# Where a tuned layer chain lets VectorE prepare its weights: a paced plan of conversions, later stores, an earlier first product

## The chip, the cores and the metric

One core of a Trainium2 chip runs the whole program. The metric is the device time of one launch in microseconds, as the median of several runs. Five compute engines work side by side: TensorE (PE, matmuls; PEld is its weight load), VectorE (DVE), ScalarE (ACT), GpSimd (POOL), and SyncE (SP), which here only issues DMAs. Each engine runs its instructions in the order in which the program emits them, so an instruction that waits holds back all behind it on its engine.

## The reference

The inputs are q, k, v of shape (4, 8, 576, 64) and the weights of two MLPs.

```python
scores = scale * np.matmul(q, k.transpose(0, 1, 3, 2))
Dmat = np.where(rel >= 0, gamma[:, None, None] ** rel[None, :, :], 0.0)
x = np.matmul(scores * Dmat, v)             # as (2304, 512): 4*576 tokens, 8*64 columns
h = x @ w_in                                # 512 -> 2048
x = (h * (1.0 / (1.0 + np.exp(-1.702 * h)))) @ w_out
h = x @ w2_in                               # 512 -> 1024
solu = h * softmax(h)
ln = (solu - mu) / np.sqrt(var + 1e-06) * g_ln
out = ln @ w2_out                           # 1024 -> 512
```

## The kernel before

**Stages.** The retention runs from 0 to 66 us in eight rounds k = 0 to 7 of two units each (a unit is a pair of heads of one batch). Then comes the first MLP in 24 steps, and from 492 us the second MLP, in which PE has no gaps.

**Numbers as pairs.** A float32 operand is held as a pair hi and lo, and a product takes three matmuls (hi·hi, lo·hi, hi·lo). `split` makes the pair: ACT casts the high part (L294 for weights, L628 for x), and POOL subtracts (L295, L630); for some of x's operands DVE subtracts (also L630).

**Products by sums.** A block product of two by two takes seven products, not eight. Their operands are sums: four of x's blocks (L285 and L621 on DVE) and four of the weights' blocks (L285, tiles t1 to t4). The results are put together by four additions with temporaries c11, c12, c21, c22 in `emit_h` (L678; copies L685 and L689 on ACT).

**Weights arrive as 64-bit words.** `convert` makes float32 of them with three DVE operations on 128x512 (L270, L273, L276). A raw slice is one DMA of SP's queue into one of two raw buffers.

**Steps.** The first MLP goes through four generations g of four slices of the hidden width, each with three pairs of token tiles and two halves i: step s = 6g + 2·(place of the pair) + i. A step is `emit_h` (seven products of six matmuls 128x384 in the order h_A, h_C, h_B, h_A, h_C, h_D, h_B, L672; `gate` gives g of h on ACT and DVE, L650 to L652) and `emit_y` (48 matmuls, 24 in steps 0 and 1, L736; added up by L745 from generation 1 on). The h products use four PSUM banks in turn, so each bank's last reader must be done before the next step's product of that name begins.

**x's operands.** A pair of tiles has seven operand tiles x0 to x6. In generation 0 the steps 1 and 3 make the next pair's (split of even j on POOL, of odd j on DVE) and store them to DRAM, xd; in the later generations steps 1 and 3 of each load them back, seven DMAs of 768 KB on ACT's queue, each after the product that frees its tile.

**The background list.** Conversions, sums and splits of weights for later steps stand in a list `bg`. `slot(n)` first runs up to three splits of the list `late` that an earlier slot took off, and then takes pieces of a summed cost of about n (a conversion operation costs 1) and emits them there. A step has one slot with a number in `emit_h`, after the adds of L678 and before the last two gates, and one after `emit_y`; the number is what is left over the slots left. At the end the list holds the second MLP's weights. `spill` splits such a slice into a park buffer (two in `ws`, three in `win[2]`) and stores it to DRAM, wd, on SP's queue, 512 KB each. After the last `emit_h`, `open_second` frees the first MLP's weights and fetches 14 slices of wd, and three more follow. `split_y` makes the second MLP's operands of the first token tiles from the finished y; in before it is called for the first pair after step 22.

**What sets the order.** There is no scheduler: the order of code is the order on each engine. The DMAs of SP and ACT share eight completion counters in turn, so a DMA also waits for the one that was issued eight places before it.

## Time and profile before

| What | Value |
|---|---|
| Runs | 692.77, 695.28, 695.31 us (median 695.28) |
| The profiled execution | 697.27 us, of it a span of 695.5 us |
| PE busy | 651.9 us, 94% |
| DVE, ACT, POOL busy | 485.6, 279.2, 213.2 us |
| Mean granted clock of PE | 0.973 |
| A step without a disturbance | 15.60 us |

The profile shows one execution. Busy times are summed per engine; since PE is busy for 94%, the places that matter are the few in which PE waits or runs at a lower clock. They lie between 66 and 112 us, near 150, 253, 350 and between 438 and 484 us.

### The profile page before, as it was taken

The numbers are of one execution on the slowest core, as the hardware profiler recorded it, in microseconds if no ns is written. First come the engines' busy times: TensorE is split into PE (matmuls) and PEld (weight loads), VectorE is DVE, ScalarE is ACT, GpSimd is POOL, SyncE is SP. The second block draws the span as 40 slices with busy tenths as digits, with TensorE's granted clock in tenths as the row PEclk, the third lists the DMA queues.
The fourth block names the chain that finished last, engine by engine and source line by source line (L and its number), as shares of the span: only waits on it lengthen the run. The fifth ranks groups of instructions, "written<-read, shape, count | busy, mean of one in ns | idle before, by whom it ended". The sixth has DMA issues, their size and how long they took to land.

```text
span 695.5 us, 11232 instructions
## 1 busy us (share of the span) xinstructions
PE 651.9 (94%) x4326; PEld 609.2 (88%) x4326; DVE 485.6 (70%) x846; ACT 279.2 (40%) x606; POOL 213.2 (31%) x216
## 2 busy tenths in 40 slices
PE   9999578989999989999999999589999999999998
PEld 8888478889999989999989999589888888888887
DVE  3897996675457766587767575565599878877780
ACT  3475344544444332333333334143354344442431
POOL 3489453540213110412111205052232234331300
PEclk9999878999999999999999999889999999999999
DMA  9997347181255762184952377767800000000001
GB/s 346 417 417 315 137 169 270 59 329 52 61 203 228 275 266 88 61 318 164 382 181 76 124 315 270 320 252 284 345 16 1 32 30 32 16 16 31 32 31 46
DMA packets 30006, 121.78 MB, mean 175 GB/s; under 512 B 3328, under 2 KB 3840, under 8 KB 29952
## 3 DMA queue, kind: packets, MB, share of 16 engines
q1 hardware_dynamic: 23760, 87.96, 33.4%
q10 hardware_dynamic: 6192, 33.10, 12.4%
q8 instruction: 34, 0.56, 0.3%
q14 instruction: 20, 0.16, 0.1%
HBM read 88.28 MB, written 32.77 MB: 174 GB/s over the span
## 4 chain that ended last, share of the span: by engine, by line
PE 68%; DMA 6%; DVE 4%; ACT 1%; issue 1%; POOL 0%; ACTq 0%; DVEq 0%
PE y L736 22%; PE o L890 14%; PE h L800 12%; PE h_B L672 5%; PE h_A L672 5%; PE h_C L672 5%; DMA x<-xd 4%; PE h_D L672 3%; PE zT L864 2%; DMA mem<-in_w2in 1%; DVE mem L273 1%; DVE mem L276 0%; DVE mem L270 0%; DVE x L630 0%; DVE g L652 0%
## 5 line engine op out<-in xcount | busy, mean ns | idle before, releaser
L295 POOL TENSOR_TENSOR win<-mem,win 128x256 fp32r<-128x256 f32 (+2 forms) x63 | 58.6, 960 | 114.7 <-ACT win L294 80.6
L736 PE MATMUL y<-g,wo 128*128 128x384 f32 x432 | 79.7, 339 | 0.0
L736 PEld LDWEIGHTS y<-g,wo 128*128 128x128 f32 x432 | 77.1, 192 | 0.3 <-DVE mem L745 0.2
L295 POOL TENSOR_TENSOR ws<-mem,ws 128x512 fp32r<-128x512 f32 (+1 forms) x28 | 32.1, 1157 | 103.0 <-ACT ws L294 103.0
L745 DVE TENSOR_TENSOR mem<-y,mem 128x384 f32<-128x384 f32 x72 | 36.7, 552 | 30.7 <-PE y L736 30.4
L678 DVE TENSOR_TENSOR mem<-h_B,mem 128x384 f32<-128x384 f32 x48 | 26.5, 551 | 32.3 <-PE h_B L672 30.2
L685 ACT COPY mem<-h_A 128x384 f32<-128x384 f32 x24 | 11.6, 483 | 84.7 <-PE h_A L672 84.7
L800 PE MATMUL h<-ut,win 128*128 128x512 f32 x168 | 42.9, 390 | 0.0
L890 PE MATMUL o<-u,zs 128*128 128x512 f32 (+1 forms) x171 | 41.7, 388 | 0.0
L736 PE MATMUL y<-g,wo1dt.float32r 128*128 128x384 f32 x216 | 40.3, 334 | 0.0
L736 PE MATMUL y<-g,wo0dt.float32r 128*128 128x384 f32 x216 | 40.3, 334 | 0.0
L806 DVE TENSOR_TENSOR mem<-h,mem 128x512 f32<-128x512 f32 x36 | 24.6, 687 | 22.4 <-PE h L800 12.5
L890 PE MATMUL o<-wo,zs 128*128 128x512 f32 (+1 forms) x171 | 40.0, 378 | 0.0
L630 POOL TENSOR_TENSOR x<-mem,x 128x384 fp32r<-128x384 f32 x30 | 34.6, 1180 | 17.5 <-ACT x L628 17.5
L736 PEld LDWEIGHTS y<-g,wo0dt.float32r 128*128 128x128 f32 x216 | 37.7, 188 | 0.0
L736 PEld LDWEIGHTS y<-g,wo1dt.float32r 128*128 128x128 f32 x216 | 37.7, 188 | 0.0
L800 PEld LDWEIGHTS h<-ut,win 128*128 128x128 f32 x168 | 31.4, 188 | 6.4
L672 PE MATMUL h_B<-x,win0dt.float32r 128*128 128x384 f32 x108 | 23.8, 358 | 13.7 <-DVE mem L678 10.8
L890 PEld LDWEIGHTS o<-wo,zs 128*128 128x128 f32 x171 | 31.0, 188 | 6.0
L276 DVE SCALAR_TENSOR_TENSOR mem<-mem 128x512 uint32<-128x512 uint32 x44 | 34.5, 785 | 1.2
L890 PEld LDWEIGHTS o<-u,zs 128*128 128x128 f32 x171 | 29.9, 189 | 5.1
L270 DVE TENSOR_SCALAR mem<-mem 128x512 uint32<-128x512 uint32 x44 | 20.7, 469 | 18.4 <-DMA mem<-in_w2in 10.6
(150 smaller groups left out, 1547.7 us busy)
## 6 DMA issues: line engine op xcount, KB each, us to landing
x<-xd ACTq DMA_DIRECT2D x42, 768.0 KB, 9.6
xd<-x SPq DMA_DIRECT2D x21, 768.0 KB, 5.3
mem<-in_w SPq DMA_DIRECT2D x28, 512.0 KB, 4.6
in<-in_att SPq DMA_DIRECT2D x16, 576.0 KB, 9.1
in<-in_att SPq DMA_DIRECT2D x16, 544.0 KB, 8.9
out<-mem SPq DMA_DIRECT2D x17, 256.0 KB, 2.0
mem<-in_w2out SPq DMA_DIRECT2D x8, 512.0 KB, 4.8
wd<-ws SPq DMA_DIRECT2D x8, 512.0 KB, 6.4
```

Source lines behind the costliest of these rows:

```text
L270: lambda: nc.vector.tensor_scalar(x, high, 3, 0x3FFFFFF8, ALU.logical_shift_left, ALU.bitwise_and),
L276: lambda: nc.vector.scalar_tensor_tensor(x, low, 29, high, ALU.logical_shift_right, ALU.bitwise_or),
L295: (engine or self.nc.gpsimd).tensor_tensor(lo, src, f32(hi), ALU.subtract)
L630: (engine or self.nc.gpsimd).tensor_tensor(x[:, 1, k], a[:, k], f32(x[:, 0, k]), ALU.subtract)
L672: nc.tensor.matmul(o, w[:, c:c + P], x[j][:, m, k], start=(start and i == 0), stop=(stop and i == 5), skip_group_check=True,)
L678: add = lambda o, a, b: nc.vector.tensor_tensor(o, a, b, ALU.add)
L736: nc.tensor.matmul(self.yps[m], w[:, c:c + P], gs[:, b], start=(begin and i == 0), stop=(end and i == 2),)
L745: nc.vector.tensor_tensor(y[:, m], self.yps[m], y[:, m], ALU.add)
L800: nc.tensor.matmul(o, a[:, l, k], w[:, m], start=(start and i == 0), stop=(stop and i == 5), skip_group_check=True,)
L806: add = lambda o, a, b: nc.vector.tensor_tensor(o, a, b, ALU.add)
L864: nc.tensor.transpose(pt[:, b * P:(b + 1) * P], u[:, w:w + P], ident)
L890: nc.tensor.matmul(o[:, 0:n], z[:, a, k], w[:, b, p * n:(p + 1) * n], start=(k == 0 and i == 0), stop=(k == FB - 1 and i == 2),)
```

## The change

Six things are changed. (1) A table `PACE` and a function `pace` give each slot its number; the slot after `emit_y` of steps 1 and 3 gets 0 in every generation, and in generation 0 the slots of step 3 both get 0. (2) `spill` no longer issues its store: it puts it in a list that the next slot runs first. (3) In the retention, the rounds 6 and 7 get a slot of 3 each, x's sums are taken in rounds 4, 5, 5 and 6 (one each in rounds 4 to 7 before), x4 is split in round 6, and the low parts of x2 and x4 are made on DVE. (4) The first product h_A of step 0 with its copy is emitted before the last `within` of round 7, and the temporaries lie elsewhere for that. (5) Before the `emit_h` of step 23 `flush` empties the list. (6) The first `split_y` goes from the end of step 22 to behind the `emit_h` and the fetches of step 23. `gate` looks up its tile later, which moves no instruction.

```diff
--- before.py
+++ after.py
@@ -1,5 +1,6 @@
 import math
 from contextlib import ExitStack
+from itertools import chain
 
 import numpy as np
 
@@ -125,6 +126,7 @@
 NPAIR = B * NP // 2
 R1_AT = _M["tmp"]
 SCAN_AT = R1_AT + 4 * NCH * CH
+SUM_AT = [SCAN_AT, SCAN_AT + TW, R1_AT, R1_AT + TW]
 
 
 RAW_AT = [_M["raw"], _M["raw"] + SLICE]
@@ -144,6 +146,7 @@
 
 WARM = 10
 LATE = 3
+PACE = ((6, 6), (6, 0), (4, 3), (0, 0), (7, 6), (7, 6))
 
 
 class Build:
@@ -166,7 +169,7 @@
         self.dram = self.pool("dram", space=bass.MemoryType.DRAM)
         self.ps = self.pool("ps", space=bass.MemoryType.PSUM)
         self.win, self.wo, self.w, self.xst = {}, {}, {}, {}
-        self.bg, self.late, self.done = [], [], set()
+        self.bg, self.late, self.stores, self.done = [], [], [], set()
         self.gfree, self.gt = list(range(8)), {}
         self.staged = set()
 
@@ -300,6 +303,9 @@
     def slot(self, n):
 
 
+        for fn in self.stores:
+            fn()
+        self.stores = []
         late, self.late = self.late[:LATE], self.late[LATE:]
         for fn, give in late:
             fn()
@@ -316,8 +322,25 @@
                 self.done.add(give)
                 n -= cost
 
+    def flush(self):
+        for _ in range(12):
+            self.slot(9)
+        assert not (self.bg or self.late or self.stores)
+
     def left(self):
         return sum(x[0] for x in self.bg)
+
+    def pace(self, s, part):
+
+
+        g, i = divmod(s, 6)
+        if g == 0:
+            return PACE[i][part]
+        slots = [(t, b) for t in range(i, 6 - (g == GENS - 1)) for b in range(2) if b == 0 or t not in (1, 3)]
+        slots = [x for x in slots if x >= (i, part)]
+        if (i, part) not in slots:
+            return 0
+        return -(-self.left() // len(slots))
 
     def queue_convert(self, raw, dst, scale=None, need=(), give=None):
         p = self.convert(raw, dst, scale)
@@ -400,7 +423,9 @@
 
         w = self.park(i)
         self.split(w[:, 0], w[:, 1], src)
-        self.nc.sync.dma_start(out=self.wd[u], in_=f32(w.rearrange("r a b -> r (a b)")))
+        self.stores.append(
+            lambda: self.nc.sync.dma_start(out=self.wd[u], in_=f32(w.rearrange("r a b -> r (a b)")))
+        )
 
     def queue_spill(self, u, src, give=None, need=()):
         i = self.spills
@@ -644,16 +669,16 @@
         nc = self.nc
         slot = self.gfree.pop(0)
         self.gt[key] = slot
-        gs = self.gs[slot]
 
         def go(h):
+            gs = self.gs[slot]
             nc.scalar.activation(gs[:, 0], h, AF.Gelu_apprx_sigmoid)
             nc.scalar.activation(h, h, AF.Gelu_apprx_sigmoid)
             nc.vector.tensor_tensor(gs[:, 1], h, f32(gs[:, 0]), ALU.subtract)
 
         return go
 
-    def emit_h(self, s, n_slot):
+    def emit_h(self, s):
 
 
         nc = self.nc
@@ -677,7 +702,7 @@
 
         add = lambda o, a, b: nc.vector.tensor_tensor(o, a, b, ALU.add)
         bank = lambda name: self.bank(f"h{s}_{name}")[:, 0:TW]
-        c11, c12, c21, c22 = (self.at(_M["tmp"] + i * TW, TW) for i in range(4))
+        c11, c12, c21, c22 = (self.at(c, TW) for c in SUM_AT)
         f = 2 * n
         g11, g12, g21, g22 = (self.gate((g, p, t, f + c)) for t in range(2) for c in range(2))
         A = bank("A")
@@ -708,7 +733,7 @@
         add(D_, D_, c21)
         add(B_, c22, c21)
         self.done.add(("h", s))
-        self.slot(n_slot)
+        self.slot(self.pace(s, 0))
         g21(D_)
         g22(B_)
         yield 6
@@ -999,7 +1024,7 @@
 
         def make_x(*js):
             for j in js:
-                split_x(j, None)
+                split_x(j, nc.vector if j in (2, 4) else None)
                 self.xready += 1
 
         self.xready = 0
@@ -1049,9 +1074,9 @@
                 self.scores(u + 1)
                 o, ends = [self.bank(f"o{u}")], [self.bank(f"e{k}")]
                 o.append(self.bank(f"o{u + 1}"))
-                if k > 3:
+                for _ in range((0, 0, 0, 0, 1, 2, 1, 0)[k]):
                     sums.pop(0)()
-                self.slot((0, 0, 3, 3, 2.4, 0, 0, 0)[k])
+                self.slot((0, 0, 3, 3, 2.4, 0, 3, 3)[k])
                 ends.append(self.ybank(f"e{u + 1}"))
                 self.across(k, o, ends, True)
                 if nxt:
@@ -1060,6 +1085,9 @@
                     self.states(u + 2, pt)
                 for i in range(2):
                     self.take(u + i, ends[i], True)
+                if not nxt:
+                    steps = self.emit_h(0)
+                    next(steps)
                 for i in range(2):
                     self.within(u + i, o[i], False)
                 if nxt:
@@ -1076,7 +1104,7 @@
             for _ in range((2, 0, 0, 1, 1, 1, 1, 0)[k]):
                 load_w()
             if k > 3:
-                make_x(*((0, 3), (1, 2), (5, 6), (4,))[k - 4])
+                make_x(*((0, 3), (1, 2), (5, 6, 4), ())[k - 4])
 
         self.open_right()
         self.slot(6)
@@ -1088,8 +1116,9 @@
             after = PAIRS[g][at + 1] if at + 1 < NPR else None
             if g == 0 and i == 0 and after is not None:
                 sums, split = self.combine_x(after)
-            slots = max(1, 2 * (5 - s % 6) + 2 - 4 * (g == GENS - 1))
-            for j in self.emit_h(s, 8.4 if s == 0 else -(-self.left() // slots) + 1):
+            if s + 1 == NSTEP:
+                self.flush()
+            for j in self.emit_h(s) if s else chain([0], steps):
                 while s == 0 and self.first_loads:
                     load_w()
                 if s == 0:
@@ -1106,11 +1135,13 @@
                 for fn in sums[:3]:
                     fn()
             if s + 1 == NSTEP:
-                self.slot(0)
-                assert not self.bg and not self.late
                 self.open_second()
                 for k, u in ((2, (1, 1)), (3, (2, 0)), (4, (2, 1))):
                     self.fetch(u, self.wo[k].rearrange("r (a b) -> r a b", a=2))
+                self.nys = 0
+                ys, y1, y2 = (self.split_y(p) for p in range(3))
+                for fn in ys:
+                    fn()
             if s < 2:
                 self.emit_y(g, p, 0, [2 * i, 2 * i + 1])
             elif i:
@@ -1119,14 +1150,7 @@
                 pg, pp, _ = STEPS[s - 1]
                 self.emit_y(pg, pp, 1, range(FG * pg, FG * pg + FG))
             self.done.add(("y", s))
-            slots -= 1
-            self.slot(6 if s == 0 else self.left() // max(1, slots) if s + 2 < NSTEP else 0)
-            if s == NSTEP - 2:
-                assert not self.bg and not self.late
-                self.nys = 0
-                ys, y1, y2 = (self.split_y(p) for p in range(3))
-                for fn in ys:
-                    fn()
+            self.slot(self.pace(s, 1))
         for fn in y1[:6] + y2[:4]:
             fn()
         self.emit_y(GENS - 1, PAIRS[-1][-1], 1, range(NF - FG, NF))
```

The line numbers move with the change: L270, L285, L294, L548, L630, L678, L685 of before are L273, L288, L297, L573, L655, L703, L710.

On DVE, at the retention's end (rounds 6 and 7; s_0_993 to s_1_1006 are round 7's scores, st the scan of states, x_130 is x4, `win1dt.uint` is where the raw words of w_out 0 and 1 lie), before:

```order
L533 TENSOR_TENSOR r_78<-e_918,mem 128x64
L533 TENSOR_TENSOR mem<-e_918,mem 128x64
L516 SCALAR_TENSOR_TENSOR st<-mem,T_946 128x512
L548 SCALAR_TENSOR_TENSOR mem<-s_0_993,mem 128x512
L548 SCALAR_TENSOR_TENSOR mem<-s_1_994,mem 128x512
L548 SCALAR_TENSOR_TENSOR mem<-s_0_1005,mem 128x512
L548 SCALAR_TENSOR_TENSOR mem<-s_1_1006,mem 128x512
L285 TENSOR_TENSOR mem<-mem 128x768
L270 TENSOR_SCALAR mem<-win1dt.uint_125 128x512
L273 SCALAR_TENSOR_TENSOR win1dt.uint_125<-win1dt.uint_125,mem 128x512
L276 SCALAR_TENSOR_TENSOR mem<-win1dt.uint_125 128x512
```

and now:

```order
L273 TENSOR_SCALAR mem<-win1dt.uint_125 128x512
L276 SCALAR_TENSOR_TENSOR win1dt.uint_125<-win1dt.uint_125,mem 128x512
L279 SCALAR_TENSOR_TENSOR mem<-win1dt.uint_125 128x512
L558 TENSOR_TENSOR r_78<-e_919,mem 128x64
L558 TENSOR_TENSOR mem<-e_919,mem 128x64
L541 SCALAR_TENSOR_TENSOR st<-mem,T_950 128x512
L655 TENSOR_TENSOR x_130<-mem,x_130 128x384 x2
L573 SCALAR_TENSOR_TENSOR mem<-s_0_1002,mem 128x512
L573 SCALAR_TENSOR_TENSOR mem<-s_1_1003,mem 128x512
L573 SCALAR_TENSOR_TENSOR mem<-s_0_1014,mem 128x512
L573 SCALAR_TENSOR_TENSOR mem<-s_1_1015,mem 128x512
```

Three conversion operations and the split of x4 (L655) came in front of round 7's four score operations; the sums of x moved to earlier rounds.

On DVE, from the y additions at the end of step 21's place in the row to the first h additions of step 22, before:

```order
L745 TENSOR_TENSOR mem<-y_1_0_3_4091,mem 128x384
L270 TENSOR_SCALAR mem<-mem 128x512
L273 SCALAR_TENSOR_TENSOR mem<-mem 128x512
L276 SCALAR_TENSOR_TENSOR mem<-mem 128x512
L270 TENSOR_SCALAR mem<-mem 128x512
L273 SCALAR_TENSOR_TENSOR mem<-mem 128x512
L276 SCALAR_TENSOR_TENSOR mem<-mem 128x512
L285 TENSOR_TENSOR mem<-mem 128x512 x2
L678 TENSOR_TENSOR mem<-h_B,mem 128x384
```

and now:

```order
L770 TENSOR_TENSOR mem<-y_1_0_3_4089,mem 128x384
L703 TENSOR_TENSOR mem<-h_B,mem 128x384
L677 TENSOR_TENSOR g_1098<-h_A,g_1098 128x384
L703 TENSOR_TENSOR h_C<-h_C,mem 128x384
L677 TENSOR_TENSOR g_1099<-h_C,g_1099 128x384
L703 TENSOR_TENSOR mem<-h_B,mem 128x384
L703 TENSOR_TENSOR h_D<-h_D,mem 128x384
L703 TENSOR_TENSOR h_B<-mem 128x384
L273 TENSOR_SCALAR mem<-mem 128x512
```

The six conversion operations and the two weight sums that stood ahead of step 22's first h addition (L678, now L703) stand behind its h additions.

On ACT, from the last gates of step 22 to the first copies of step 23 (`ws` and `win_1073`, `win_1090` are the park buffers; the seven casts of 128x256 belong to `split_y`), before:

```order
L650 ACTIVATE g_1086<-h_B 128x384
L651 ACTIVATE h_B<-h_B 128x384
L294 CAST win_1073<-mem 128x512
L294 CAST ws<-mem 128x512 x2
L294 CAST win_1073<-mem 128x256 x7
L685 COPY mem<-h_A 128x384
L689 COPY mem<-h_C 128x384
L650 ACTIVATE g_1083<-h_A 128x384
L651 ACTIVATE h_A<-h_A 128x384
```

and now:

```order
L675 ACTIVATE g_1103<-h_B 128x384
L676 ACTIVATE h_B<-h_B 128x384
L297 CAST ws<-mem 128x512 x2
L297 CAST win_1090<-mem 128x512 x3
L297 CAST ws<-mem 128x512 x2
L710 COPY mem<-h_A 128x384
L714 COPY mem<-h_C 128x384
L675 ACTIVATE g_1100<-h_A 128x384
L676 ACTIVATE h_A<-h_A 128x384
```

Four more casts into park buffers stand ahead of step 23's first copy of h_A, and the seven casts of `split_y` are gone from there.

## Rows read from the trace of the kernel before

**Rows 1.** The page: span, and the additions of y (last: out<-in xcount | busy, mean ns).

```profile
span 695.5 us, 11232 instructions
...
L745 DVE TENSOR_TENSOR mem<-y,mem 128x384 f32<-128x384 f32 x72 | 36.7, 552 | 30.7 <-PE y L736 30.4
```

**Rows 2.** Windows: from:to length, busy of PE, PEld, DVE, ACT, POOL, PEclk, DMA, GB/s.

```profile
48.00:66.07 18.07, 15.47 (x340) 14.24 (x333) 12.76 (x20) 11.98 (x29) 18.07 (x17) 1.00 0.83 339
66.07:85.21 19.14, 12.54 (x69) 11.30 (x67) 17.82 (x27) 8.18 (x17) 9.14 (x8) 0.95 0.44 182
85.21:111.88 26.67, 18.45 (x67) 17.15 (x68) 24.58 (x29) 11.98 (x23) 17.11 (x13) 0.69 0.59 220
```

**Rows 3.** PE in time: start, us, instruction, [idle before it <- who ended it].

```profile
85.21 0.69 PE L672 MATMUL h_A<-x,win1dt.float32r 128*128 128x384 f32 x1 [5.03 <-ACT win1dt.float32r L294]
88.51 1.97 PE L672 MATMUL h_A<-x,win1dt.float32r 128*128 128x384 f32 x5 [2.62 <-POOL win1dt.float32r L295]
...
99.90 1.87 PE L672 MATMUL h_B<-x,win1dt.float32r 128*128 128x384 f32 x6 [2.73 <-DVE mem L678]
```

**Rows 4.** DVE in time, retention's end and step 1.

```profile
62.22 2.70 DVE L548 SCALAR_TENSOR_TENSOR mem<-s,mem 128x512 f32<-128x512 f32 x4
...
96.48 2.90 DVE L630 TENSOR_TENSOR x<-mem,x 128x384 fp32r<-128x384 f32 x2
...
101.10 1.02 DVE L630 TENSOR_TENSOR x<-mem,x 128x384 fp32r<-128x384 f32 x2
```

**Rows 5.** Windows of steps 4, 7 and 10.

```profile
146.26:166.60 20.34, 17.46 (x91) 17.14 (x91) 15.66 (x29) 9.47 (x22) 4.12 (x4) 0.92 0.58 195
197.80:213.40 15.60, 15.60 (x91) 15.60 (x91) 9.42 (x19) 7.01 (x15) 3.70 (x3) 1.00 0.84 334
244.60:264.61 20.01, 17.65 (x92) 17.07 (x91) 10.55 (x21) 5.43 (x12) 2.77 (x2) 0.91 0.69 255
```

**Rows 6.** PE in time, the waits of steps 4, 10 and 16.

```profile
151.38 2.11 PE L672 MATMUL h_B<-x,win0dt.float32r 128*128 128x384 f32 x6 [2.88 <-DVE g L652]
...
250.83 1.28 PE L672 MATMUL h_D<-x,win 128*128 128x384 f32 x6 [0.86 <-DMA x<-xd]
...
253.60 1.90 PE L672 MATMUL h_B<-x,win 128*128 128x384 f32 x6 [1.49 <-DMA x<-xd]
...
350.68 1.28 PE L672 MATMUL h_B<-x,win1dt.float32r 128*128 128x384 f32 x6 [1.66 <-DMA x<-xd]
```

**Rows 7.** DVE in time, a conversion operation ahead of step 3's last gates.

```profile
148.38 0.69 DVE L273 SCALAR_TENSOR_TENSOR mem<-mem 128x512 uint32<-128x512 uint32 x1
```

**Rows 8.** Windows of steps 22 and 23.

```profile
438.33:466.34 28.01, 17.81 (x92) 17.20 (x92) 14.58 (x26) 8.30 (x17) 9.40 (x7) 0.82 0.65 267
466.34:483.54 17.20, 15.89 (x91) 15.57 (x91) 8.23 (x18) 6.41 (x17) 4.88 (x7) 1.00 0.73 260
```

**Rows 9.** PE in time, steps 22 and 23.

```profile
444.29 1.28 PE L672 MATMUL h_D<-x,win0dt.float32r 128*128 128x384 f32 x6 [0.60 <-DMA x<-xd]
...
455.18 2.29 PE L672 MATMUL h_B<-x,win0dt.float32r 128*128 128x384 f32 x6 [9.60 <-DVE mem L678]
...
470.93 1.34 PE L672 MATMUL h_A<-x,win1dt.float32r 128*128 128x384 f32 x6 [1.31 <-ACT mem L685]
```

**Rows 10.** DVE, ACT and POOL in time, step 22.

```profile
448.71 0.43 DVE L270 TENSOR_SCALAR mem<-mem 128x512 uint32<-128x512 uint32 x1 [8.46 <-DMA mem<-in_w2in]
...
455.75 1.28 POOL L295 TENSOR_TENSOR win<-mem,win 128x512 fp32r<-128x512 f32 x1
...
460.77 1.15 ACT L294 CAST ws<-mem 128x512 fp32r<-128x512 f32 x2
```

**Rows 11.** DMAs issued at 434.15, 429.88 and 455.81: size in KB, us to landing.

```profile
x<-xd ACTq DMA_DIRECT2D x1, 768.0 KB, 13.1
...
wdt<-ws SPq DMA_DIRECT2D x1, 512.0 KB, 8.2
...
wdb<-ws SPq DMA_DIRECT2D x1, 512.0 KB, 2.6
```

## The prediction

> **What bounds the kernel now.** I read first the page's share of PE, 94%: over most of the program PE is the bound, and a DVE that works less gives nothing there. So the time can only come out of stretches in which PE waits or has its lower clock. To find them I read PE in time, from step to step, against the step without a disturbance: step 7 takes 15.60 us, and PE is busy for all of it at a granted clock of 1.00 [rows 5]. Steps 0 and 1 have 66 matmuls and not 90, so 15.60 · 66/90 = 11.44 us is their share. Above these lie: step 0 by 19.14 − 11.44 = 7.7, step 1 by 26.67 − 11.44 = 15.2 [rows 2], step 4 by 4.74, step 10 by 4.41 [rows 5], step 16 by at least its wait of 1.66 [rows 6], step 22 by 12.41, step 23 by 1.60 [rows 8]. All the rest of the program I take as unchanged.
>
> Then I asked of each place what ended the wait. At step 1 it is the weights of win1, cast on ACT (5.03 us) and subtracted on POOL (2.62), then an addition on DVE (2.73) [rows 3]; DVE is busy for 17.82 + 24.58 of the 45.81 us there, so behind those names DVE is the bound. At step 4 it is the last gates on DVE, at steps 10 and 16 loads of x's operands [rows 6], at step 22 an addition on DVE that stands behind conversions, which wait 8.46 us for a raw slice [rows 9, 10].
>
> **The retention's end and steps 0 and 1.** The change does two opposite things here. It adds two pairs of subtractions (x2, x4) to DVE; a pair takes 1.02 us alone and 2.90 beside POOL's work [rows 4], so 2.0 to 5.8, and I take the middle, 3.9. And it moves six conversion operations into rounds 6 and 7, in which DVE has 18.07 − 12.76 = 5.3 us free [rows 2]; about half of that lies in front of operations that wait for PE's own results, so I take 2.7 as filled. Third, of the conversions in step 1 three stand no longer ahead of the split of x1 and of the first h addition; the wait of 2.73 that this addition ends [rows 3] goes. The sum is 3.9 − 2.7 − 2.7 = **−1.5**. Bounds: +5.8 if nothing is filled and nothing goes; 2.0 − 5.3 − 2.7 = −6.0 if all does. The cover is thin: round 7's scores, at 62.22 before [rows 4], now stand behind x4's split, this behind its cast on ACT, this behind the cast of w_out 0, and this behind three conversion operations. PE's `within` of round 7 waits for the scores, and only the first product h_A (1.2 us) fills that; e, the bank of the last tokens, is also late. The DMAs of the split pairs stay where they were: x's stores are issued in step 0.
>
> On the pair's price the trace shows 1.02 and 2.90 us for the same shape, and POOL busy for 18.07 of 18.07 us at the retention's end [rows 2, 4]. The Trainium skill (SBUF — State Buffer, "Who interferes with whom") says that a DVE operation with two inputs in SBUF and a GpSimd operation that reads SBUF exclude each other for a whole instruction, and this speaks against moving x2 and x4 to DVE. By that rule both pairs would cost 2.90, 1.9 more than I take, and the sum would end at −10.4; the two rows agree with it, but the moved subtractions also leave POOL, so I keep the middle.
>
> **Step 4.** The third product waits 2.88 us for a gate of step 3 [rows 6]. Four conversion operations (0.69 us for the longer ones [rows 7]) stand ahead of step 3's last gates; `pace` takes them away. What is then late is ACT's part of the same gate, about 1 us earlier: the wait falls to some 1.9. The other 4.74 − 2.88 = 1.86 us of this step are a stretch at lower clock behind that wait (0.92 in the window [rows 5]); I let half of it go. **−2.0**, bounds −4.7 (all of it) and 0.
>
> **Steps 10 and 16.** Two loads of x's operands come late, 0.86 and 1.49 us, and the lower clock behind them is the rest, 4.41 − 2.35 = 2.06 [rows 5, 6]. The loads of steps 7 and 9 are the same seven; behind step 7 none is late, with 334 GB/s in its window [rows 5]. What is added in step 9 are a raw slice and a parked store. With the slot behind step 9's y at 0 and stores one slot later, one of each leaves the stretch in which x5 and x6 travel. I take the whole: **−4.4** and for step 16 **−1.7**; bounds 0 for both, if what leaves at the step's end was not what the loads shared the queues with.
>
> **Step 22.** The wait of 9.60 us [rows 9] goes from this place: the first h addition is now ahead of the conversions, so their 8.46 us for a raw slice [rows 10] run beside PE. What is late next are x5 (0.60 [rows 9]) and x6: issued at 434.15, 13.1 us to landing [rows 11], so at 447.25, when the product before it, h_D from 444.29, has needed about 1.05 us: 447.25 − 445.35 = 1.9. With it goes a stretch of lower clock of about the size of step 10's, 2.06. So 0.6 + 1.9 + 2.1 = 4.6 remain of 12.41: **−7.8**. Bounds: −12.4 if x6 comes in time, −4 if it lands 4 us later since the store that its issue waits for does (that store takes 8.2 us [rows 11]).
>
> **Step 23.** Here the change adds a wait. `flush` puts the last splits at the start of the step, and seven casts stand on ACT ahead of the copy of h_A; behind this copy are the copy of h_C, all gates of the step, and on PE the fourth product, which writes the same bank. The last cast (t4) needs the park buffer of b22, whose store must have landed. From the step's start: two y additions 1.1 [rows 1], a conversion operation 0.7 [rows 7], a cast 0.58, POOL 1.28 [rows 10], the store 2.6 [rows 11], the cast 0.58, the copy some 0.5: 7.3 us. PE needs it after three products, at about 3.1. That is a wait of 4.2 to 4.7 (some issue between), and with 2.1 of lower clock 6.7 above the undisturbed step, where 1.60 stood (the wait of 1.31 [rows 9]): **+5.1**. Bounds: 0, if the store is earlier than the start, and +10.7, if it takes 8.2 and not 2.6. `split_y` costs nothing more: its splits come behind step 23's h and have the y part, some 8 us, as cover. The fetches stand behind the last stores on SP's queue and have until the second MLP starts; I see no wait there.
>
> The park stores issued one slot later hold back no engine but SP, where raw loads are now ahead of them; this is the gain at step 22 and is not counted twice.
>
> **The sum.** −1.5 − 2.0 − 4.4 − 1.7 − 7.8 + 5.1 = −12.3 us. The profiled execution took 697.27, which gives 685.0; it stands 2.0 above the median of the runs, 695.28, and against that the forecast is **683.0 us**.
>
> **Rivals.**
> The start pays in full: DVE has win1 ready when step 0's y ends, and the waits 5.03, 2.62 and 2.73 [rows 3] go, 10.4 us in place of 1.5. Sum −21.2: 674.1. For it speaks that POOL loses four of the subtractions it had in rounds 5 to 7; against it that nine conversion operations then stand ahead of step 0's first h addition.
> The loads stay late: `pace` empties only the slot behind y of the loading steps; the one in their `emit_h` still gives conversions, with a raw load and a store each. Then steps 10 and 16 keep their 6.1 us: −6.2, 689.1. This is the case in which the change does half of what it says.
> The retention's tail decides, on the slower side: everything that was put ahead of round 7's scores is on the path, 5.8 for the pairs, 3 · 0.69 for the conversions, 0.6 for the cast, 8.5 us, and while PE stands still its clock falls; step 1, entered after waits of 5.03 and 2.62, had 0.69 and PE busy for 18.45 us for 11.44 of work [rows 2, 3], so some 6 us more in step 0. 14.5 − 10.8 (the other terms) = +3.7: 699.0. It turns the sign when tail and clock pass 10.8 us.
>
> **How the numbers follow.** Forecast 0.50, start pays 0.17, loads stay late 0.20, tail 0.08, other ways 0.05. The range reaches from the start's case (674) to above the case of the loads (692), which leaves out the tail and some of the others, about 0.15 to 0.2. A measurement of this kernel tells some 0.5% from no change, 3.5 us: faster means below 691.8. Forecast and start lie wholly there or nearly, and most of the loads' case: 0.78. Slower is the tail: 0.08. The rest, 0.14, is the same.
>
> **What would show it.** In the profile of the changed kernel: PE's wait ahead of h_A in step 1 no longer than about 7 us; h_B of step 4 with under 2 us; no x<-xd ahead of a product in steps 10 and 16; in step 22 no wait for an addition but one of about 2 us for x6; in step 23 a wait of over 4 us ahead of the second h_A, ended by the copy on ACT. I would be wrong on the sign if PE stands still for over 10 us between 62 us and the first h_C. I would be wrong on the size if step 23's wait is 10 us, or if the fetches make the second MLP start late.

## The result, and the profile after

The changed kernel takes 699.47 us (median of 18 runs, 694.78 to 702.66), the kernel before 695.88 us beside it (18 runs, 691.92 to 698.94). The ratio is 1.0051, with an interval of 1.0026 to 1.0075: slower by some 3.6 us (1.8 to 5.2). The forecast was 683.0 us with a range from 674 to 692, so it was wrong, and in its sign.

The profiled execution of the changed kernel took 697.27 us with a span of 695.5 us, the same as that of before. It is one of its quicker executions. A second one of each was profiled: 700.85 us for the changed kernel, 698.06 us for the kernel before. The table sets all four side by side, from the starts of PE's first product of each step; all steps not in it take 15.6 to 16.2 us in all four.

| Stretch, us | before | before, again | after | after, again | mean change | forecast |
|---|---|---|---|---|---|---|
| Start of step 2 | 111.88 | 112.11 | 114.01 | 115.35 | +2.7 | −1.5 |
| Steps 2 and 3 | 34.38 | 33.68 | 33.58 | 34.50 | 0.0 | 0 |
| Step 4 | 20.34 | 21.63 | 18.80 | 20.05 | −1.6 | −2.0 |
| Step 10 | 20.01 | 18.32 | 21.13 | 21.09 | +1.9 | −4.4 |
| Step 16 | 17.51 | 17.52 | 20.81 | 21.17 | +3.5 | −1.7 |
| Step 22 | 28.01 | 29.09 | 18.39 | 18.18 | −10.3 | −7.8 |
| Step 23 and the last y part | 25.72 | 25.71 | 30.84 | 30.85 | +5.1 | +5.1 |
| Second MLP starts at | 492.06 | 492.82 | 491.76 | 495.36 | +1.1 | −12.3 |

The gain at step 22 is there, and larger than forecast; the price at step 23 is there, to the tenth. What failed are two terms: the retention's end, and above all the loads of steps 10 and 16. Where the second MLP starts, the two kernels differ by 1.1 us in the mean of their two profiles, not by 3.6. Both profiled executions of the kernel before (697.27 and 698.06 us) were slower than its median of 695.88, and those of the changed kernel lie on both sides of its own. So much of the rest is what the kernel before gains in its quicker executions, and no trace shows where.

The waits of PE in the profile of after, in time (start, us, instruction, idle before it and what ended it), at the retention's end and in step 1, to be read against [rows 3]:

```profile
71.75 0.38 PE L604 MATMUL e<-in,st 64*64 64x64 f32 x2 [4.16 <-DVE mem L573]
...
77.50 1.31 PE L697 MATMUL h_C<-x,win0dt.float32r 128*128 128x384 f32 x6
...
88.87 0.45 PE L697 MATMUL h_A<-x,win1dt.float32r 128*128 128x384 f32 x1 [0.69 <-ACT win1dt.float32r L297]
91.92 1.97 PE L697 MATMUL h_A<-x,win1dt.float32r 128*128 128x384 f32 x5 [2.60 <-POOL win1dt.float32r L298]
...
101.90 1.34 PE L697 MATMUL h_B<-x,win1dt.float32r 128*128 128x384 f32 x6 [1.24 <-DVE mem L703]
```

The 5.03 us ahead of step 1 went to 0.69, as one would wish, but a new wait of 4.16 us stands in round 7, and h_C of step 0 begins at 77.50, where it began at 67.25. The same view for the later waits, against [rows 6, 9]:

```profile
150.95 1.32 PE L697 MATMUL h_B<-x,win0dt.float32r 128*128 128x384 f32 x6 [1.11 <-DVE g L677]
...
251.71 1.31 PE L697 MATMUL h_D<-x,win 128*128 128x384 f32 x6 [1.81 <-DMA x<-xd]
254.79 2.26 PE L697 MATMUL h_B<-x,win 128*128 128x384 f32 x6 [1.78 <-DMA x<-xd]
...
350.38 1.29 PE L697 MATMUL h_D<-x,win1dt.float32r 128*128 128x384 f32 x6 [1.50 <-DMA x<-xd]
353.43 2.26 PE L697 MATMUL h_B<-x,win1dt.float32r 128*128 128x384 f32 x6 [1.76 <-DMA x<-xd]
...
448.42 1.30 PE L697 MATMUL h_D<-x,win0dt.float32r 128*128 128x384 f32 x6 [0.52 <-DVE g L677]
451.45 1.30 PE L697 MATMUL h_B<-x,win0dt.float32r 128*128 128x384 f32 x6 [1.73 <-DMA x<-xd]
469.09 2.20 PE L697 MATMUL h_A<-x,win1dt.float32r 128*128 128x384 f32 x6 [4.89 <-ACT mem L710]
```

In steps 10 and 16 the loads are later than before, not earlier; step 16 has a second wait, and behind it a product at half speed (2.26 us, where 1.2 is usual), which it had not before. Step 22 keeps x6's 1.73 and 0.52 for a gate, and step 23 has the new 4.89 ahead of the second h_A.

### The profile page after: what moved, and what is told of

It is laid out like the page before. It is cut to its first block, busy times and chain, and to the rows that moved or that the text cites. A ratio compares the mean times of both kernels' runs of the same rounds, so it can differ in the third digit from the quotient of the medians.

```text
span 695.5 us, 11230 instructions
## 1 busy us (share of the span) xinstructions
PE 654.2 (94%) x4326; PEld 610.5 (88%) x4326; DVE 494.2 (71%) x850; ACT 279.7 (40%) x606; POOL 209.4 (30%) x212
## 4 chain that ended last, share of the span: by engine, by line
PE 62%; DMA 8%; issue 5%; DVE 2%; ACT 2%; POOL 1%; ACTq 0%; POOLq 0%; DVEq 0%
PE y L761 19%; PE o L915 14%; PE h L825 12%; PE h_B L697 4%; PE h_A L697 4%; PE h_C L697 4%; DMA x<-xd 4%; DMA mem<-in_w2out 3%; PE zT L889 2%; PE h_D L697 2%; DMA wdt<-ws 1%; POOL ws L298 1%; DVE mem L770 1%; DVE x L655 0%; ACT g L675 0%
## 5 line engine op out<-in xcount | busy, mean ns | idle before, releaser
L298 POOL TENSOR_TENSOR win<-mem,win 128x256 fp32r<-128x256 f32 (+2 forms) x63 | 60.5, 992 | 107.3 <-ACT win L297 103.2
L761 PE MATMUL y<-g,wo 128*128 128x384 f32 x432 | 78.3, 335 | 0.0
L761 PEld LDWEIGHTS y<-g,wo 128*128 128x128 f32 x432 | 75.6, 189 | 0.3 <-DVE mem L770 0.2
L703 DVE TENSOR_TENSOR mem<-h_B,mem 128x384 f32<-128x384 f32 x48 | 26.5, 552 | 37.2 <-PE h_B L697 33.3
L710 ACT COPY mem<-h_A 128x384 f32<-128x384 f32 x24 | 11.6, 485 | 86.7 <-PE h_A L697 86.7
L831 DVE TENSOR_TENSOR mem<-h,mem 128x512 f32<-128x512 f32 x36 | 24.6, 688 | 22.1 <-PE h L825 12.5
L279 DVE SCALAR_TENSOR_TENSOR mem<-mem 128x512 uint32<-128x512 uint32 x44 | 35.6, 809 | 1.0
L655 POOL TENSOR_TENSOR x<-mem,x 128x384 fp32r<-128x384 f32 x26 | 30.8, 1209 | 16.8 <-ACT x L653 16.7
L276 DVE SCALAR_TENSOR_TENSOR mem<-mem 128x512 uint32<-128x512 uint32 x44 | 34.0, 773 | 1.4
L288 DVE TENSOR_TENSOR mem<-mem 128x256 f32<-128x256 f32 (+2 forms) x49 | 31.9, 685 | 2.8 <-POOL x L655 1.9
```

Source lines behind the costliest of these rows:

```text
L276: lambda: nc.vector.scalar_tensor_tensor(high, high, 0xC0000000, x, ALU.bitwise_and, ALU.bitwise_or),
L279: lambda: nc.vector.scalar_tensor_tensor(x, low, 29, high, ALU.logical_shift_right, ALU.bitwise_or),
L288: self.nc.vector.tensor_tensor(o, a, b, ALU.subtract)
L298: (engine or self.nc.gpsimd).tensor_tensor(lo, src, f32(hi), ALU.subtract)
L655: (engine or self.nc.gpsimd).tensor_tensor(x[:, 1, k], a[:, k], f32(x[:, 0, k]), ALU.subtract)
L703: add = lambda o, a, b: nc.vector.tensor_tensor(o, a, b, ALU.add)
```

## The experiments

### The retention's end, put back or changed in parts

Theory: what was put ahead of round 7's scores delays step 0 more than the earlier conversions give back. The rival was that they pay and the loss lies elsewhere. First the whole of it as before:

```diff
-                split_x(j, nc.vector if j in (2, 4) else None)
+                split_x(j, None)
-                for _ in range((0, 0, 0, 0, 1, 2, 1, 0)[k]):
+                for _ in range((0, 0, 0, 0, 1, 1, 1, 1)[k]):
-                self.slot((0, 0, 3, 3, 2.4, 0, 3, 3)[k])
+                self.slot((0, 0, 3, 3, 2.4, 0, 0, 0)[k])
-                if not nxt:
-                    steps = self.emit_h(0)
-                    next(steps)
-            for j in self.emit_h(s) if s else chain([0], steps):
+            for j in self.emit_h(s):
-                make_x(*((0, 3), (1, 2), (5, 6, 4), ())[k - 4])
+                make_x(*((0, 3), (1, 2), (5, 6), (4,))[k - 4])
-PACE = ((6, 6), ...
+PACE = ((8.4, 6), ...
```

> The changed kernel with the retention's end of the kernel before: x2 and x4 subtracted on POOL, no slots in rounds 6 and 7, one sum a round, the first product behind round 7; everything else as changed. Theory tail: what was put ahead of round 7's scores delays the first h_C by 10 us and the win1 that is ready earlier gives back less; then step 2 begins 2 us earlier than in the changed kernel (about 112.0 and not 114.0), and the time is about 2 us under it. Rival, that the conversions moved forward do pay and the loss lies elsewhere: step 2 begins at 114 or later, the time is the same or worse.

Measured: step 2 begins at 112.06, the ratio to the kernel before is 1.0007 (0.9981 to 1.0033), so the retention's part of the change costs about 2 us in the profile and 0.44% (3 us) of the changed kernel's time, just clear of the noise of the two ratios. The rival falls. The first profile shows this price at its smallest: seven of the profiled executions run the changed kernel's code up to step 5, which begins at 166.3 to 171.8 us (168.75 in the mean), and step 4 takes 18.7 to 18.8 us in three of them and 20.0 to 21.6 in four. With the retention's end of before, step 5 begins at 164.53, and step 4 takes 18.79. Two parts of the edit alone follow: x2 and x4 back on POOL (the first of the edits above), and no slots in rounds 6 and 7 (the third and the last).

> The changed kernel with x2 and x4 subtracted on POOL again. Theory lock (the pairs on DVE cost 2.2 to 2.5 us each ahead of the scores): the scores of round 7 begin at about 66.5 to 67 and not at 70.95, step 1 gets its weights some 3 to 4 us earlier, and step 2 begins at about 111. Rival cast (x4's split only waits where the cast of w_out 0, the copies and three x casts on ACT hold it, and POOL would do them no earlier for PE): the scores begin earlier all the same, but x4 then comes late on POOL for h_C of step 0, which waits, and step 2 begins at 113 to 114.

Measured: ratio 1.0037 (1.0016 to 1.0059), which is not told from the changed kernel's; step 2 begins at 112.97. The scores begin at 68.23, later than the theory had it, and h_C of step 0 does not wait for x4, against the rival. What holds the scores is something else. DVE in time, of this kernel:

```profile
64.18 0.96 DVE L288 TENSOR_TENSOR mem<-mem 128x768 f32<-128x768 f32 x1 [7.36 <-POOL x L655]
...
68.23 2.70 DVE L573 SCALAR_TENSOR_TENSOR mem<-s,mem 128x512 f32<-128x512 f32 x4
```

A sum of x that overwrites what x2 is split from waits 7.36 us for POOL. So the earlier sums need x2 on DVE; without it they make a new wait.

> The changed kernel without the conversions in rounds 6 and 7 of the retention (they come in step 0, as in the kernel before); x2 and x4 stay on DVE, the first product stays early. Theory conversions: the three operations of w_out 0, 4.2 us long beside POOL, and its cast ahead of the copies on ACT are the larger part of the tail; without them round 7's scores begin at about 66 to 67 and not at 70.95, h_C at 72 to 73 and not at 77.5; but the conversions then come after and step 2 begins at 112 to 114, the time within 0.3% of the changed kernel's. Rival pairs: the scores stay behind 69, since x4's split waits for its cast.

Measured: the scores begin at 66.58 and h_C at 72.58, so the conversions were the larger part of the tail, as the theory said: in the changed kernel they and w_out 0's cast stand like this (DVE, then ACT, in time):

```profile
60.67 1.49 DVE L273 TENSOR_SCALAR mem<-win1dt.uint 128x512 uint32<-128x512 uint32 x1
62.19 1.37 DVE L276 SCALAR_TENSOR_TENSOR win1dt.uint<-win1dt.uint,mem 128x512 uint32<-128x512 uint32 x1
63.59 1.37 DVE L279 SCALAR_TENSOR_TENSOR mem<-win1dt.uint 128x512 uint32<-128x512 uint32 x1
...
68.82 2.21 DVE L655 TENSOR_TENSOR x<-mem,x 128x384 fp32r<-128x384 f32 x2 [2.46 <-ACT x L653]
70.95 2.71 DVE L573 SCALAR_TENSOR_TENSOR mem<-s,mem 128x512 f32<-128x512 f32 x4
```

```profile
65.00 0.62 ACT L297 CAST wo0dt.float32r<-mem 128x512 fp32r<-128x512 f32 x1 [5.58 <-DVE mem L279]
65.52 1.07 ACT L621 COPY mem<-o 128x512 f32<-128x512 f32 x2
66.48 2.31 ACT L653 CAST x<-mem 128x768 fp32r<-128x768 f32 x3
```

The three operations take 4.2 us there, beside POOL; the next three, which start at 73.59 when POOL is still, take 1.8. ACT stands still for 5.58 us for the first three, and behind ACT x4's split, the scores, and PE. But without them the ratio is 1.0058 (1.0033 to 1.0083), the same as with them: the 5.03 us that the kernel before has ahead of step 1 come back as 4.46. Early or late, these operations are on the path here; the early place only chooses which wait it is. Neither part alone gives the 3 us back, so how they divide among the parts of this edit is not shown.

### The company of the loads

Theory: the stretch in which x's operands are loaded is bound by the DMA engines, and each transfer of SP's queue in it delays x6. The rival was that each load takes its 3.1 us in any case. The edit takes the conversions, and with them raw loads and stores, out of this stretch in generations 1 and 2:

```diff
-... for t in range(i, 6 - (g == GENS - 1)) for b in range(2) if b == 0 or t not in (1, 3)]
+... for t in range(i, 6 - (g == GENS - 1)) for b in range(2)
+    if ((t, b) not in ((2, 1), (3, 0), (3, 1)) if g < GENS - 1 else b == 0 or t not in (1, 3))]
```

> The changed kernel with a plan that in generations 1 and 2 gives no conversions to step 3 of a generation and to the slot behind y of step 2, and gives them to the slot behind y of step 1 again. So one or two transfers of SP's queue share the time with the loads of x's operands in steps 9 and 15, and not five. Theory bandwidth (the stretch moves about 360 GB/s with whatever is in it, so each 512 KB costs x6 some 1.45 us): x6 lands 4 to 6 us earlier, the waits of 1.81 and 1.78 in step 10 and of 1.50 and 1.76 in step 16 go, both steps take 15.6 to 16 us, the time falls by 9 to 10.5. Rival ring (x's loads come one behind the other on ACT's queue and each takes some 3.1 us in this generation whatever SP does): the waits stay over 1 us each, under 2 us of gain.

Measured: steps 10 and 16 take 15.60 and 15.60 us, without any wait. The rival falls. The DMA view from x0's issue in step 9 to x6's landing (packets and mean rate; then packets, MB and share of SP's queue q1; then issues with their median time to landing), of the kernel before (23.2 us long):

```profile
DMA packets 1676, 8.00 MB, mean 345 GB/s; under 512 B 176, under 2 KB 176, under 8 KB 1673
...
q1 hardware_dynamic: 665, 2.46, 25.9%
```

of the changed kernel (24.6 us):

```profile
DMA packets 1731, 8.16 MB, mean 332 GB/s; under 512 B 192, under 2 KB 192, under 8 KB 1728
...
q1 hardware_dynamic: 720, 2.62, 27.8%
...
mem<-in_w2out SPq DMA_DIRECT2D x2, 512.0 KB, 10.1
wd<-ws SPq DMA_DIRECT2D x2, 512.0 KB, 7.8
mem<-in_w SPq DMA_DIRECT2D x1, 512.0 KB, 9.8
```

and of the experiment (18.1 us):

```profile
DMA packets 1120, 5.92 MB, mean 327 GB/s; under 512 B 128, under 2 KB 128, under 8 KB 1117
...
q1 hardware_dynamic: 109, 0.38, 6.3%
```

The rates lie within 5% of each other, 327 to 345 GB/s; what differs most is what goes through. From 18.1 to 24.6 us for 2.24 MB more on SP's queue is 1.5 us for each 512 KB (0.524 MB). And in the changed kernel there is not less of it than before but more. For the loads of step 15 it is one transfer, before (22.3 us long):

```profile
DMA packets 1592, 7.64 MB, mean 342 GB/s; under 512 B 177, under 2 KB 177, under 8 KB 1591
...
q1 hardware_dynamic: 583, 2.12, 23.3%
```

and in the changed kernel (24.1 us):

```profile
DMA packets 1729, 8.14 MB, mean 338 GB/s; under 512 B 192, under 2 KB 192, under 8 KB 1728
...
q1 hardware_dynamic: 720, 2.62, 28.3%
```

For those of step 9 it is only 0.16 MB, about 0.5 of the 1.4 us; the rest is the lower mean rate, whose cause no run shows. x6's load is issued 2.8 us later there too (242.09, 239.32 before), but x5's, issued at 235.60 (235.90 before), already lands 0.9 us later, so the late issue is not what starts the delay. The reason for the company is in the list: the slot behind y of step 7 gets 0 as well, so everything behind it comes later by three operations, and the raw slice that was issued at 225.27, ahead of the loads, is now issued at 231.65, 1.5 us behind x0. From the start of step 6 to the end of step 8 DVE begins 12 conversion operations, where it was 15 before, and in step 9 nine, where it was six.

The time, though, did not fall by the 9 to 10.5 us of the theory: it was 1.0064 (1.0038 to 1.0090), and steps 12 and 18 take 20.54 and 19.61. PE in time in step 12, then ACT and DVE at the end of step 11:

```profile
282.71 1.31 PE L697 MATMUL h_B<-x,win1dt.float32r 128*128 128x384 f32 x6 [1.95 <-DVE g L677]
289.56 1.34 PE L697 MATMUL h_B<-x,win1dt.float32r 128*128 128x384 f32 x6 [2.41 <-DVE mem L703]
```

```profile
274.97 0.62 ACT L297 CAST ws<-mem 128x512 fp32r<-128x512 f32 x1 [6.72 <-DMA wd<-ws]
```

```profile
276.39 0.56 DVE L677 TENSOR_TENSOR g<-h_C,g 128x384 fp32r<-128x384 f32 x1 [7.36 <-ACT h_C L676]
```

There are nine slots a generation where the changed kernel has ten, and the work comes closer together. In step 11 two casts into the park buffers `ws` follow each other, and the second waits 6.72 us for a store out of `ws` to land. Behind it on ACT stand the gates of step 11, so the gate on DVE waits 7.36 us, and h_B of step 12 on PE waits for that. In step 17 the same cast waits 6.71. The second wait of step 12 has five conversion operations ahead of its addition on DVE. The work can be moved, but it needs a place with room, on DVE and in the park buffers.

### Step 22 and step 23

What took 9.6 us off step 22, the order on DVE or the later stores? The first edit uses the slots behind y of steps 19 and 21 again:

```diff
-... if b == 0 or t not in (1, 3)]
+... if b == 0 or t not in ((1, 3) if g < GENS - 1 else ())]
```

> The changed kernel with the slots behind y of steps 19 and 21 used again in the last generation. Theory order on DVE: what took 9.6 us off step 22 is that no conversion stands between the y additions and the first h addition of step 22; with four of them back there, which wait for raw slices, step 22 has a wait for DVE ahead of its last h_B of 3 to 9 us again. Rival: the wait went because the stores are issued later and the raw slices so come earlier; then step 22 stays at 18.4 to 20.5 us.

The second lets the stores go at once:

```diff
-        self.stores.append(
-            lambda: self.nc.sync.dma_start(out=self.wd[u], in_=f32(w.rearrange("r a b -> r (a b)")))
-        )
+        self.nc.sync.dma_start(out=self.wd[u], in_=f32(w.rearrange("r a b -> r (a b)")))
```

> The changed kernel with the stores of parked slices issued at their split again. Theory company: it is the number of transfers beside the loads that counts, and a store one slot earlier is still beside them; steps 10 and 16 stay at 20.5 to 21.5 us, step 22 within 2 us of 18.4 to 20.5, and the time is the same within 0.3%. Rival head of the queue: a store that waits for its split holds the raw loads behind it on SP's queue, so step 22 has a wait for conversions again, over 4 us more there.

With conversions back in front of its first addition step 22 takes 22.46 us; PE in time:

```profile
457.72 2.29 PE L697 MATMUL h_B<-x,win0dt.float32r 128*128 128x384 f32 x6 [3.94 <-DVE mem L703]
```

The wait for DVE is back, so it is the order that took it away. It is less than 9.60: four conversions stand ahead of the addition, where it was six and two sums, and the raw slice keeps DVE waiting for 6.75 us, where it was 8.46 [rows 10]. The ratio is 1.0089 (1.0065 to 1.0114), 2.6 us above the changed kernel's. With stores at once, steps 10, 16 and 22 take 21.32, 20.90 and 19.91, as the theory had it, and the wait in step 23 is 5.54; this explains 2 to 3 us. But the ratio is 1.0157 (1.0125 to 1.0189), 7 us above the changed kernel's. The profiled execution, 700.26, was the quickest of four (up to 709.76), so where the others lose the rest no trace shows. The theory's 0.3% fails; that the later store is worth something is measured, why so much stays open.

For step 23, the list is emptied two products later:

```diff
-            if s + 1 == NSTEP:
-                self.flush()
             for j in self.emit_h(s) if s else chain([0], steps):
+                if s + 1 == NSTEP and j == 1:
+                    self.flush()
```

> The changed kernel with the list emptied behind the copies of h_A and h_C of step 23 and not ahead of them. Theory order on ACT: the wait of 4.89 us ahead of the second h_A (ended by the copy on ACT) and the lower clock behind it go, step 23 falls from 22.3 to about 15.6 to 17 us, the time by 5 to 6.5. Rival: the same casts then stand ahead of the gate of h_A and the addition of h_C waits no less, or the fetches begin later and the second MLP waits for them: under 2 us of gain.

Measured: 1.0014 (0.9987 to 1.0042), 2.6 us under the changed kernel, between the theory's 5 to 6.5 and the rival's under 2. From step 23's start to the second MLP's first product it takes 26.72 us (469.12 to 495.84), 4.1 less. The wait for the copy is gone; a wait of 2.28 for an addition took part of its place, since the list's operations on DVE now stand ahead of that:

```profile
477.81 1.31 PE L697 MATMUL h_B<-x,win1dt.float32r 128*128 128x384 f32 x6 [2.28 <-DVE mem L703]
```

And `split_y` put back ahead of the products of step 23:

```diff
             if s + 1 == NSTEP:
                 self.flush()
+                self.nys = 0
+                ys, y1, y2 = (self.split_y(p) for p in range(3))
+                for fn in ys:
+                    fn()
...
-                self.nys = 0
-                ys, y1, y2 = (self.split_y(p) for p in range(3))
-                for fn in ys:
-                    fn()
             if s < 2:
```

> The changed kernel with the first split_y behind the emptied list and ahead of the products of step 23, where the kernel before had it. Seven more casts (0.4 to 0.5 us each) then stand on ACT ahead of the copy of h_A. Theory order on ACT: the wait ahead of the second h_A grows from 4.9 by 2 to 4 us. Rival: the casts wait for nothing and fill the time in which ACT waits for the store of b22; the wait grows by under 1 us.

Measured: 1.0114 (1.0084 to 1.0144), and PE in time:

```profile
476.96 2.29 PE L697 MATMUL h_A<-x,win1dt.float32r 128*128 128x384 f32 x6 [9.84 <-ACT mem L710]
```

The wait grows by 4.95, more than the theory's 4. The seven casts take 2.54 us, and between them ACT waits 1.46 for a subtraction of `split_y` on DVE and 0.94 for two stores out of the park buffers that they write, as ACT in time shows (the first wait, 1.83, is 1.81 in the changed kernel too):

```profile
470.98 0.62 ACT L297 CAST ws<-mem 128x512 fp32r<-128x512 f32 x1 [1.83 <-DMA wdb<-ws]
...
473.05 0.71 ACT L297 CAST win<-mem 128x256 fp32r<-128x256 f32 x2 [1.46 <-DVE mem L791]
473.99 0.71 ACT L297 CAST win<-mem 128x256 fp32r<-128x256 f32 x2 [0.23 <-DMA wdt<-win]
475.41 1.12 ACT L297 CAST win<-mem 128x256 fp32r<-128x256 f32 x3 [0.71 <-DMA wdb<-win]
476.43 0.47 ACT L710 COPY mem<-h_A 128x384 f32<-128x384 f32 x1
```

So this move, which I gave no price, is worth 4 to 5 us where the change puts `flush`.

### Once more, and what is better than both

> The kernel before once more, for how much one profiled execution differs from another: steps 4, 10, 16 and 22 within 3 us of 20.3, 20.0, 17.5 and 28.0. Where steps 10 and 16 of this execution are as long as in the changed kernel (about 21), the loss there is less than the two profiles say.

> The changed kernel once more, for how much one profiled execution differs from another: step 2 begins at 114 to 116, steps 4, 10, 16 and 22 take 18.8 to 21.6, 20.7 to 22, 20.8 to 21.9 and 18.4 to 20.5 us, as the unchanged parts of the other kernels do; the place that differs tells where the median lies above the first profiled execution.

They are the columns of the first table. Steps 10 and 16 of the kernel before are 18.32 and 17.52 in the second execution, so the loss there is real. In the second execution of the changed kernel step 1's last product waits 4.67 us for DVE, where the first waited 1.24.

If the three losses are what they seem, they can be taken off: the edits of the old retention and of the later `flush`, and a plan in which only step 3 of a generation is empty:

```diff
-... if b == 0 or t not in (1, 3)]
+... if (t != 3 if g < GENS - 1 else b == 0 or t not in (1, 3))]
```

> Three things at once: the retention's end of the kernel before, the list emptied behind the copies of h_A and h_C in step 23, and a plan that in generations 1 and 2 gives no conversions to step 3 of a generation and gives them to the slot behind y of step 1 again. If the three losses of the changed kernel are the tail, the loads' company and the order on ACT, they add up: step 2 begins at about 112, steps 10 and 16 take 15.6 to 17.5 us (three to four transfers share the time with the loads, where five did), step 23 some 4 us less, and the time is about 684 to 688, faster than before by 1 to 1.6%. If the plan only moves the waits to the steps behind (20 us in steps 12 and 18, as a plan with one slot fewer had it), it is 692 to 696.

Measured: 688.99 us against 697.01 beside it, ratio 0.9889 (0.9867 to 0.9911): the losses add up, though the time is a little above the 684 to 688 hoped for, since step 10 still takes 18.82. Then half a slot less behind y of step 2, and `flush` one product later still (j == 2):

```diff
-        return -(-self.left() // len(slots))
+        return -(-self.left() // len(slots)) / (2 if (i, part) == (2, 1) and g < GENS - 1 else 1)
```

> The kernel with the three things undone or mended (688.99 us), with half the conversions in the slot behind y of step 2 of generations 1 and 2, and with the list emptied one product later in step 23. One transfer fewer beside the loads is worth 1.2 to 1.5 us of x6's landing each time, so steps 10 and 16 fall from 18.8 and 17.3 to 15.6 to 17; the wait of 2.28 us for an addition on DVE in step 23 goes. Expected 684 to 687. If the slots behind grow too heavy, steps 11, 12, 17 or 18 get waits of 0.5 to 2 us, and the time is 688 to 691.

Measured: 685.97 us against 697.42, ratio **0.9835** (0.9811 to 0.9859), the fastest kernel here. Step 10 takes 17.23 us, and steps 11 to 18 take 15.91 at most. In step 23 the wait moved once more, behind the h products:

```profile
469.92 6.20 PE L761 MATMUL y<-g,wo 128*128 128x384 f32 x24 [3.27 <-DVE mem L770]
```

but from its start to the second MLP it is 29.24 us (450.88 to 480.12), 1 more than in the kernel before it (453.49 to 481.73, 28.24), so this second edit lost what it was to gain.

## Why the prediction was wrong, step by step

**The reading of the bound** held: the places that matter were the ones named, and nothing else moved.

**The retention's end** (−1.5, measured +2.7). The pairs cost 2.53 and 2.21 us, 4.7 and not 3.9. The step that failed is the filling: I counted 2.7 us of free time on DVE as gained, with no row behind the half that I took, but DVE's free time there is free since ACT and PE are in a chain with it, and operations put into it push that chain. The measured gain is nothing: without the conversions in rounds 6 and 7 the ratio is 1.0058, with them 1.0051. I had written this chain down and priced it, as the rival of the tail: 8.5 us against 8.73 measured at the scores (62.22 to 70.95). But I gave it 0.08. That the sums agree is partly luck: the conversions took 4.2 us where 2.1 were put, the pairs 4.7 where 5.8 were. The rival's second half, 6 us of lower clock, did not come like this: `within` took 2.96 for 1.97 and h_A 2.29 for 1.2, about 2 us, and from h_C on the clock was full. That half was mis-sized by a stretch of step 1 taken for step 0. And most of the delay did not last: h_C of step 0 begins 10.25 us later, step 1 only 3.66 and step 2 only 2.13, since the 5.03 us ahead of step 1, which I had left standing, went to 0.69. So the rival's 699.0 us is near the measured 699.47 by luck.

The third term failed too, the wait of 2.73 in step 1 that was to go. In the first profile it shrank to 1.24, but the wait for w_out 3 behind it grew by more than that; in the second it was 4.67. That later wait, before and in the changed kernel:

```profile
105.54 0.45 PE L736 MATMUL y<-g,wo3dt.float32r 128*128 128x384 f32 x1 [0.67 <-ACT wo3dt.float32r L294]
```

```profile
107.69 0.69 PE L761 MATMUL y<-g,wo3dt.float32r 128*128 128x384 f32 x1 [2.37 <-ACT wo3dt.float32r L297]
```

**Steps 10 and 16** (−6.1, measured +5.4). This step failed in its sign, and it is most of the error: the waits for loads grew from 2.35 to 3.59 us in step 10 and from 1.66 to 3.26 in step 16. I looked at which transfers leave the stretch when step 9's slot is emptied. I did not follow the list: emptying step 7's slot moves all that follows back, and so a raw slice from ahead of the loads into them. The order of code was there to be read. The rival of the late loads had the right place, but it stopped at "keeps its 6.1 us"; that the change could add to them was in no bound, and that is why the range missed too.

**Step 4** (−2.0, measured −1.6): right in mechanism; the wait fell from 2.88 to 1.11, a little more than expected, and a wait of 1.52 for the copy of h_A appeared in its step. The size is less sure: over the seven executions of this code the step takes 20.0 us in the mean, 1.0 less than before.

**Step 22** (−7.8, measured −10.3): the mechanism was right. The remainder, 4.6 us, was too large, since the lower clock did not come (1.00 in the window of the changed kernel); where I had put 0.6 for x5, a gate cost 0.52. The windows of steps 22 and 23 of the changed kernel (from:to, length, busy of PE, PEld, DVE, ACT, POOL, granted clock, DMA, GB/s), against [rows 8]:

```profile
442.53:460.92 18.39, 16.14 (x92) 15.54 (x91) 11.33 (x23) 5.00 (x11) 1.43 (x1) 1.00 0.69 282
460.92:483.25 22.33, 17.44 (x92) 17.12 (x92) 13.57 (x23) 10.03 (x23) 12.05 (x11) 0.92 0.71 274
```

**Step 23** (+5.1, measured +5.1): right in mechanism and size; 4.89 of wait where 4.2 to 4.7 was worked out.

**The lock of DVE and GpSimd.** The Trainium skill's rule (SBUF — State Buffer, "Who interferes with whom"), which I had set against the middle price, would have each pair pay the 2.90 us of the row beside POOL; the traces gave 2.53 and 2.21, nearer to that than to the 1.02 alone. Beside POOL the conversion operations, to which I had not applied it, slow down more: three take 4.2 us, and 1.8 without POOL.

## What to carry to other kernels

When a slot of a background list is emptied, follow the whole list: everything behind it comes later, and a transfer that had been ahead of a critical stretch can slide into it. Idle time of an engine is only room if nothing in the chain behind it starts from the operation that the filler pushes; look for who waits for the engine next, on its partners too. And a delay at one place is not yet its price at the end: follow it to the next wait that it can hide, as the 10.25 us at h_C came down to 2.13.

## What the runs showed of the hardware

A second short wait can cost more than its length. In step 16 of the kernel before there is one wait of 1.66 us, and the product behind it takes 1.28 us [rows 6]. In the changed kernel there are waits of 1.50 and 1.76 us some 3 us apart, and the product takes 2.26 at a granted clock of 0.50, so the step has 20.81 − 15.60 − 3.26 = 1.95 us beyond its waits. It is no fixed price: without the conversions in rounds 6 and 7, step 10 had waits of 1.68 and 1.75 us and its product took 1.30. Two executions of the changed kernel show it in step 4, with the same waits (1.11 or 1.09, and these) but not the same product behind the second:

```profile
153.78 1.32 PE L697 MATMUL h_A<-x,win0dt.float32r 128*128 128x384 f32 x6 [1.52 <-ACT mem L710]
```

```profile
156.03 2.29 PE L697 MATMUL h_A<-x,win0dt.float32r 128*128 128x384 f32 x6 [1.50 <-ACT mem L710]
```

The loads' stretch moved 327 to 345 GB/s with 0.38 MB of SP's queue in it or 2.62, so there the landing of a load follows from the bytes to some 5%.
